# Seven block products for eight in a pooled-attention and feed-forward kernel, with the second weight matrix read from DRAM at every step

## The chip, the cores and the metric

The kernel runs on one core of a Trainium2 chip. The metric is the device time of one execution in microseconds (us); the time of a kernel is the median of several executions. Engines are named as the profile names them: PE is TensorE's matrix array, PEld its weight loads, DVE VectorE, ACT ScalarE, POOL GpSimd, SP SyncE, which issues all DMAs here.

## What is computed

Attention over keys and values that are averaged in groups of eight, then a feed-forward layer with a squared ReLU:

```python
k_p = k.reshape(B, H, Sp, pool, D).mean(axis=3)      # B, H, S, D = 8, 8, 576, 64; pool = 8
v_p = v.reshape(B, H, Sp, pool, D).mean(axis=3)
scores = scale * np.matmul(q, k_p.transpose(0, 1, 3, 2))
...
x = np.ascontiguousarray(attn_out.transpose(0, 2, 1, 3)).reshape(B * S, H * D)   # 4608 x 512
h = np.maximum(x @ w_in, 0.0)                        # w_in 512 x 2048
return (h * h @ w_out)                               # w_out 2048 x 512
```

All tensors are float32. The weights arrive as 64-bit numbers, which the kernel converts itself.

## The kernel before

The 4608 tokens are cut into 12 chunks of 384 (`CH`). A chunk has 16 steps (`NFC`), one for each block of 128 hidden units. One step multiplies the chunk's x by one block of w_in (`hidden`: 12 matmuls of 128x128 weights with 384 columns, tiles h), takes ReLU and square into r (`activate`), splits r into a high and a low float32r part (`split_hidden`: gh by a cast on ACT, gl by a subtraction on DVE), and multiplies the parts of two steps ago (`LAG`) by a block of w_out into three banks o that collect a whole chunk (`project`: 9 matmuls of 512 columns, three for each bank). Every float32 product of chunks 1 to 11 is made of three float32r products: high x high, high x low, low x high. That is why h reads xh and xl, and both halves of a weight tile w_i. Both weight matrices stay in SBUF, in 33 tiles of the tag "w".

After the last step of a chunk `store` copies the three banks through tiles ob (`OB`, 3 buffers) and sends them out.

The attention of the next chunk runs beside that, in four pairs of heads, p = 0 to 3, each a sequence of stages: `turn_q`, `split_q` (tiles st: two casts on ACT, two subtractions on DVE), `scores` (tiles sps on PE, copied to sc by ACT, the column maximum mx by POOL), `exponents` (subtraction, Exp on ACT, the sums tot by POOL), four small DMAs that turn the sums into reciprocals rb (rs, rc, rr, rd), and `weigh_values` (av on PE, scaled by rb on DVE, split into xh and xl). A table gives the step of each stage: `STEADY` holds the first step of each pair of heads, counted from the chunk's own first step, and the distances of the nine stages.

Engines run in the order in which the loop at the end of the program records instructions: for a step first `hidden`, then the attention's matmuls, `project`, `split_hidden`, the remaining stages of the table, the loads, and last `activate` and `store`. Nothing is reordered afterwards. An instruction that waits therefore holds up everything behind it on its engine. SP is such a queue too. The lines to find are `split_q` (L375), `scores` (L384), `exponents` (L409), `hidden` (L552), `split_hidden` (L579), `project` with `store` (L589) and the loop (L740).

Of the kernel before, what the change touches and what calls it, by code (L numbers as in the profile page):

```python
# [37 lines left out]
def pooled_attn_relu2_ffn(  # L38
# [45 lines left out]
    SPLIT = 6  # L84


    STEADY = ((-22, -18, -14, -10), (-1, 0, 1, 3, 4, 5, 6, 7, 8))
    KV0 = -39
    EARLY = ((-16, -13, -10, -7), (0, 1, 2, 3, 5))

    NKT = H * SP_ // QT
# [422 lines left out]

    x0 = []

    def split_x0():
        xts[0] = [sb.tile([P, NPAIR, CH], F32R, name=f"{x}_0", tag=x, bufs=2) for x in ("xh", "xl")]
        for i, x in enumerate(x0):
            split(*(t[:, 2 * i:2 * i + 2] for t in xts[0]), x)  # L520

    def weigh_values(c, p):

        if p == 0 and c == 0:
            x0.extend(w_tile(F32, f"x_{c}_{i}")[:, :, :CH] for i in range(2))
# [26 lines left out]
    def hidden(c, fc):  # L552
        hp = ps_h.tile([P, 512], F32, name=f"h_{c}_{fc}", tag="h")
        cb, o = fc * P // WC, fc * P % WC
        prods = []
        for cc in range(NCC):
            key, cols = ("i", cb, cc // 2 * 2), slice(cc % 2 * WC + o, cc % 2 * WC + o + P)
            if c == 0 and fc < SPLIT:
                prods += [(wf[key][:, cols], x0[cc // 2][:, cc % 2, :])]
            else:  # L560
                prods += [(wt[key][:, w, cols], xts[c][x][:, cc, :]) for w, x in ((0, 0), (0, 1), (1, 0))]
        for i, (w, x) in enumerate(prods):
            PE.matmul(hp[:, :CH], lhsT=w, rhs=x, start=i == 0, stop=i == len(prods) - 1)
# [23 lines left out]
    accs = {}  # L587

    def project(c, fc):  # L589
        if fc == 0:  # L590
            accs[c] = [ps_o.tile([P, 512], F32, name=f"o_{c}_{t}", tag=f"o{t}") for t in range(NTT)]
        g, key = gts.pop((c, fc)), ("o", fc)
        for t in range(NTT):
            tt = slice(t * P, (t + 1) * P)
            if c == 0:
                prods = [(g[:, tt], wf[key])]
            else:
                prods = [(g[x][:, tt], wt[key][:, w, :]) for x, w in ((0, 0), (0, 1), (1, 0))]
            for i, (a, w) in enumerate(prods):
                PE.matmul(accs[c][t], lhsT=a, rhs=w, start=fc == 0 and i == 0, stop=fc == NFC - 1 and i == len(prods) - 1)  # L600

        def store():
# [5 lines left out]
        return store if fc == NFC - 1 else None  # L608


    steps = [(c, fc) for c in range(NCH) for fc in range(NFC)]
# [99 lines left out]
    def kv_steps(b, s):
# [9 lines left out]
    ready = {0, 1}  # L721
    stages = (turn_q, split_q, scores, exponents, send_sums, fetch_sums, reciprocals, fetch_reciprocals, weigh_values)
    for c in range(1, NCH):
        first, offsets = EARLY if c == 1 else STEADY
        names = (transpose_q, token_scores, token_normalise, token_turn, weigh_values) if c == 1 else stages
        for b, _, _ in segments(c):
            if b not in ready:
# [7 lines left out]
                at(s + d, f, c, p)  # L735


    last = (to_float32, split_weights)
    on_pe = (transpose_k, transpose_q, scores, token_scores, token_turn, weigh_values)
    for s in range(-PRO, len(steps) + LAG):  # L740
        todo = work.get(s, [])
        activate = hidden(*steps[s]) if 0 <= s < len(steps) else None
        later = [f(*a) for f, a in sorted(((f, a) for f, a in todo if f in on_pe), key=lambda x: x[0] is weigh_values)]
        store = project(*steps[s - LAG]) if s >= LAG else None
        if 0 <= s - 1 < len(steps):
            split_hidden(*steps[s - 1])
# [12 lines left out]
        for f in (activate, store):  # L759
            if f:  # L760
                f()

# [29 lines left out]
```

## Time and profile before

| | |
|---|---|
| median of 3 executions | 944.36 us (944.16 to 945.4) |
| the profiled execution | 946.16 us |
| its span, first to last instruction | 944.4 us |
| mean granted clock of TensorE | 0.997 |
| matmuls, weight loads | 4776, 4776 |
| DMA | 68.06 MB, 72 GB/s on average |

The page gives busy time by engine, then groups of instructions: operation, output<-inputs, shape, count | busy us, mean ns of one | idle time of the engine ahead of them and what ended it. The chain lists what ended last, in order of time. In a table of windows each row is a stretch of time with the busy us of PE, PEld, DVE, ACT and POOL, the granted clock, the DMA engines' share and GB/s. All work is recorded through one helper, L34, so groups are told apart by their tiles.

### The profile page before, as it was taken

To read this page: it belongs to the slowest core of one execution; us is meant where nothing else is said; L and a number is where in the kernel's file an instruction comes from. 1 tells how busy PE (TensorE), PEld (TensorE's weight loads), DVE (VectorE), ACT (ScalarE), POOL (GpSimd) and SP (SyncE) were. 2 spreads that over 40 slices of the span, in tenths; PEclk is the share of its full clock that TensorE was granted. 3 is DMA by queue.
4 is the path that set the end of the run, shared out by engine and by line. 5 is a ranking of instruction groups with operands and counts; after the bars stand their busy time and mean duration, and the time that the engine had idled before them with its cause. 6 is when DMAs were issued, how large, how long until landed. Compare 5 with 4: busy or idle time off the path is not lost.

```text
span 944.4 us, 13423 instructions
## 1 busy us (share of the span) xinstructions
PE 929.4 (98%) x4776; PEld 785.4 (83%) x4776; DVE 598.3 (63%) x1020; ACT 434.4 (46%) x903; POOL 352.9 (37%) x215
## 2 busy tenths in 40 slices
PE   7899999999999999999999999999999999999998
PEld 6556668888888888888888888888888888888997
DVE  7988896766655576776765576676765555553221
ACT  3888766654434344344435334434434443432222
POOL 3820144435344443534443443435344443530000
PEclk9999999999999999999999999999999999999999
DMA  9975213223112113223211023223311101100000
GB/s 258 319 241 144 73 40 104 60 69 99 43 30 68 36 50 95 68 73 87 63 36 52 19 68 87 51 75 91 70 41 40 53 18 28 50 10 10 34 1 33
DMA packets 124682, 68.06 MB, mean 72 GB/s; under 512 B 95800, under 2 KB 105224, under 8 KB 124616
## 3 DMA queue, kind: packets, MB, share of 16 engines
q1 hardware_dynamic: 124616, 67.22, 26.3%
q8 instruction: 37, 0.61, 0.3%
q14 instruction: 29, 0.24, 0.1%
HBM read 55.73 MB, written 11.45 MB: 71 GB/s over the span
## 4 chain that ended last, share of the span: by engine, by line
PE 88%; DMA 4%; DVE 3%; POOL 2%; ACT 2%; issue 1%; SPq 0%; DVEq 0%; ACTq 0%
PE o L34 41%; PE h L34 40%; PE av L34 3%; PE sps L34 3%; POOL v L34 2%; DMA k<-in_k_dram 1%; DMA v<-in_v_dram 1%; DVE wf_o L34 1%; DVE wf_i L34 1%; POOL vp L34 1%; DMA raw_i<-in_moe_w_in_dram 1%; DMA vv<-in_v_dram 1%; DVE tm L34 1%; ACT te L34 1%; DVE w_i L34 0%
## 5 line engine op out<-in xcount | busy, mean ns | idle before, releaser
L34 PE MATMUL h<-xh,w_i 128*128 128x384 f32 x1488 | 417.1, 341 | 0.0
L34 PE MATMUL o<-w_o,gh 128*128 128x512 f32 x1056 | 333.9, 397 | 0.0
L34 PEld LDWEIGHTS h<-xh,w_i 128*128 128x128 f32 x1488 | 272.6, 188 | 10.7 <-issue 2.2
L34 POOL PARTITION_ALL_REDUCE tot<-sc x80 | 202.2, 2574 | 188.6 <-issue 178.4
L34 PE MATMUL h<-xl,w_i 128*128 128x384 f32 x744 | 249.8, 336 | 0.0
L34 PEld LDWEIGHTS o<-w_o,gh 128*128 128x128 f32 x1056 | 193.1, 188 | 51.6 <-issue 16.5
L34 POOL PARTITION_ALL_REDUCE mx<-sc x80 | 114.8, 1483 | 285.3 <-ACT sc L34 279.3
L34 DVE TENSOR_TENSOR gl<-r,gh 128x384 fp32r<-128x384 f32 x176 | 137.0, 779 | 114.4 <-ACT gh L34 114.4
L34 PE MATMUL o<-w_o,gl 128*128 128x512 f32 x528 | 208.8, 395 | 0.0
L34 DVE TENSOR_TENSOR r<-r 128x384 f32<-128x384 f32 x160 | 100.8, 630 | 132.8 <-ACT r L34 131.0
L34 ACT ACTIVATE r<-h 128x384 f32<-128x384 f32 x192 | 94.4, 492 | 136.0 <-PE h L34 135.0
L34 ACT CAST gh<-r 128x384 fp32r<-128x384 f32 x176 | 90.4, 514 | 130.3 <-DVE r L34 129.8
L34 PEld LDWEIGHTS h<-xl,w_i 128*128 128x128 f32 x744 | 139.7, 188 | 10.6 <-issue 3.1
L34 PEld LDWEIGHTS o<-w_o,gl 128*128 128x128 f32 x528 | 99.1, 188 | 22.2
L34 ACT CAST xh<-rb 128x384 fp32r<-128x384 f32 x40 | 20.5, 513 | 120.2 <-DVE rb L34 120.2
L34 ACT ACTIVATE sc<-sc 72x384 f32<-72x384 f32 x80 | 39.7, 525 | 47.0 <-DVE sc L34 47.0
L34 DVE TENSOR_TENSOR rb<-av,rb 128x384 f32<-128x384 f32 x40 | 22.3, 557 | 40.5 <-PE av L34 40.5
L34 DVE TENSOR_TENSOR st<-qt,st 64x384 fp32r<-64x384 f32 x80 | 44.2, 553 | 3.5 <-ACT st L34 1.0
L34 ACT COPY sc<-sps 72x384 f32<-72x384 f32 x80 | 34.1, 477 | 26.6 <-PE sps L34 26.6
L34 PE MATMUL av<-sc,vp 72*64 72x384 f32 (+1 forms) x256 | 43.8, 426 | 2.3 <-ACT sc L34 2.3
L34 PE MATMUL o<-wf_o,r 128*128 128x512 f32 x96 | 44.6, 601 | 0.0
L34 DVE TENSOR_REDUCE kp<-k 96x64 f32<-96x512 f32 x42 | 43.6, 1038 | 0.1
(82 smaller groups left out, 709.6 us busy)
## 6 DMA issues: line engine op xcount, KB each, us to landing
k<-in_k_dram SPq DMA_DIRECT2D x48, 192.0 KB
out_dram<-ob SPq DMA_DIRECT2D x36, 256.0 KB
raw_i<-in_moe_w_in_dram SPq DMA_DIRECT2D x16, 512.0 KB
raw_o<-in_moe_w_out_dram SPq DMA_DIRECT2D x16, 512.0 KB
rb<-rd SPq DMA_DIRECT2D x80, 96.0 KB
v<-in_v_dram SPq DMA_DIRECT2D x36, 192.0 KB
q<-in_q_dram SPq DMA_DIRECT2D x112, 48.0 KB
q<-in_q_dram SPq DMA_DIRECT2D x96, 24.0 KB
```

Source lines behind the costliest of these rows:

```text
L34: return lambda *a, **k: self.tc.keep_in_program_order(f(*a, **k))
```

## The change

From chunk 3 (`SC`) on the product of w_in and x is made by Strassen's scheme in Winograd's form. The weights are four blocks A11, A12, A21, A22 (halves of the hidden units by halves of the model dimension), x four blocks B11 to B22 (halves of the model dimension by halves of the chunk's tokens, 192 columns each). Seven block products take the place of eight: A11·B11, A12·B21, S2·T2, S1·T1, S3·T3, S4·B22, A22·T4, where S1 to S4 are sums of weight blocks and T1 to T4 differences of x blocks. A block product is six matmuls of 192 columns (`product`). Two steps together make one pair q: 128 hidden units of the first half and 128 of the second. `first_half` has four products, `second_half` three. Results are gathered in r1 and r2: partial sums stay in the PSUM banks pc (chain), pd and pe, and ACT and DVE copy and add between products.

The sums S are built once, in steps 30 to 57, and stay in SBUF (16 tiles). For them the parts of w_out move out: `evict` writes each of the 16 tiles to DRAM, and from chunk 2 (`MC`) on `stream` reads the one that a step needs, two steps ahead, 512 KB each. `project` runs three steps behind from chunk 2 on, and its three thirds, one for each bank, are put between the products. The differences T and the splits of the seven operands stand in the last three steps ahead of a chunk and in its first. In `exponents` the subtraction moves from DVE to POOL for chunks from 3 on. The stages of the attention move two steps earlier, ob has two buffers for three, and the tag "w" 32 for 33.

```diff
-    LAG, QL = 2, 5
+    HB = CH // 2
+    NQD = NFC // 2
+    SC, MC = 3, 2
+    LAG, FLAG, QL = 2, 3, 5
...
-    STB, SCB, LD, OB = 1, 2, 4, 3
+    STB, SCB, LD, OB, XB, KPB = 1, 2, 4, 2, 8, 2
+    BUILD, RING = (30, 37, 44, 51), 2
...
-    STEADY = ((-22, -18, -14, -10), (-1, 0, 1, 3, 4, 5, 6, 7, 8))
+    STEADY = ((-24, -20, -16, -12), (-1, 0, 1, 3, 4, 5, 6, 7, 8))
...
-        return wts.tile([P, 2, 512], dt, name=name, tag="w", bufs=2 * NFC + 1)
+        return wts.tile([P, 2, 512], dt, name=name, tag="w", bufs=2 * NFC)
...
-            DVE.tensor_tensor(sc[:, i], sc[:, i], mx[i], op=ALU.subtract)
+            (GP if c >= SC else DVE).tensor_tensor(sc[:, i], sc[:, i], mx[i], op=ALU.subtract)
...
+            if c >= SC:
+                DVE.tensor_tensor(xf[c][p // 2][:, p % 2, :], av[:, :CH], rb, op=ALU.mult)
+                return
...
+        elif name == "T2":
+            GP.tensor_tensor(tmp[c], block(c, "B22"), tmp[c], op=ALU.subtract)
...
+    def operand(c, name):
+        src = {"T1": tmp.get(c), "T2": tmp.get(c), "T3": block(c, "B12"), "T4": block(c, "B21")}.get(name)
+        t = ops[c, name] = x_tile(f"{name}_{c}").rearrange("p x (a n) -> p x a n", a=2)
+        split(t[:, 0], t[:, 1], block(c, name) if src is None else src)
...
+    def product(c, q, w, x, bank, start):
+        g, o = q // 2, q % 2 * P
+        t = wt[("s", int(w[1]), g) if w[0] == "S" else ("i", g + 4 * (w[1] == "2"), 2 * (w[2] == "2"))]
+        prods = [(t[:, i, k * WC + o:k * WC + o + P], ops[c, x][:, j, k, :])
+                 for k in range(2) for i, j in ((0, 0), (0, 1), (1, 0))]
+        for i, (a, b) in enumerate(prods):
+            PE.matmul(bank[:, :HB], lhsT=a, rhs=b, start=start and i == 0, stop=i == len(prods) - 1,
+                      skip_group_check=not start)
...
+    def parts(c, f):
...
+        split(gh, gl, gts[c, f])
...
+    def rest(c, q):
+        r2 = gts[c, q + NQD]
+        ACT.activation(r2[:, HB:], r2[:, HB:], AF.Relu)
+        ACT.activation(r2, r2, AF.Square)
+        parts(c, q + NQD)
+
+    def first_half(c, q, before, out_groups, on_array):
+        chain = ps_h.tile([P, 512], F32, name=f"pc_{c}_{q}", tag="h")
+        product(c, q, "A11", "B11", chain, True)
+        r1 = result_tile(c, q)
+        ACT.copy(r1[:, :HB], chain[:, :HB])
+        if before:
+            parts(*before)
+        next(out_groups, None)
+        other = ps_h.tile([P, 512], F32, name=f"pd_{c}_{q}", tag="h")
+        product(c, q, "A12", "B21", other, True)
+        DVE.tensor_tensor(r1[:, :HB], other[:, :HB], r1[:, :HB], op=ALU.add)
+        product(c, q, "S2", "T2", chain, False)
+        ACT.copy(r1[:, HB:], chain[:, :HB])
+        last = ps_a.tile([P, 512], F32, name=f"pe_{c}_{q}", tag="a")
+        product(c, q, "S1", "T1", last, True)
+        r2 = result_tile(c, q + NQD)
+        ACT.copy(r2[:, HB:], last[:, :HB])
+        next(out_groups, None)
+        later = on_array()
+        next(out_groups, None)
+        if before:
+            rest(*before)
...
+    def second_half(c, q, out_groups, on_array):
+        chain, last, r1, r2 = quads.pop((c, q))
+        product(c, q, "S3", "T3", chain, False)
+        DVE.tensor_tensor(r2[:, HB:], chain[:, :HB], r2[:, HB:], op=ALU.add)
+        later = on_array()
+        next(out_groups, None)
+        next(out_groups, None)
+        product(c, q, "S4", "B22", last, False)
+        next(out_groups, None)
+        product(c, q, "A22", "T4", chain, False)
+
+        def finish():
+            DVE.tensor_tensor(r1[:, HB:], last[:, :HB], r1[:, HB:], op=ALU.add)
+            DVE.scalar_tensor_tensor(r1, r1, 0.0, r1, op0=ALU.max, op1=ALU.mult)
+            ACT.activation(r2[:, :HB], chain[:, :HB], AF.Relu)
...
+    def evict(f):
+        d = scratch[f] = dram.tile([P, 2, 512], F32, name=f"wd_{f}", tag=f"wd_{f}", bufs=1)
+        load(d, wt["o", f].bitcast(F32))
+
+    def stream(c, f):
+        t = streamed[c, f] = w_tile(F32R, f"ws_{c}_{f}")
+        load(t.bitcast(F32), scratch[f])
...
+        w_o = wf[key] if c == 0 else wt[key] if c < MC else streamed.pop((c, fc))
...
+    for s, (c, f) in projects.items():
+        if c >= MC:
+            at(s - RING, stream, c, f)
+    for g, s in enumerate(BUILD):
+        for stage in range(7):
+            at(s + stage, build, g, stage)
+    for c in range(SC, NCH):
+        s = c * NFC
+        for d, f, name in ((-9, difference, "T1"), (-3, operand, "B11"), (-3, difference, "T3"), (-2, operand, "B21"),
+                           (-2, operand, "T1"), (-2, difference, "T2"), (-1, operand, "T2"), (-1, operand, "T3"),
+                           (-1, operand, "B22"), (-1, difference, "T4"), (0, operand, "T4")):
+            at(s + d, f, c, name)
```

On PE a step of before, here the second of chunk 6, starts with the 12 matmuls of h; w_i are tiles of w_in, xh and xl the parts of x:

```order
L34 MATMUL h_6_1_5130<-xh_6_4457,w_i_0_0_1309 128x384 [waits Activation_49]
L34 MATMUL h_6_1_5130<-xl_6_4458,w_i_0_0_1309 128x384
L34 MATMUL h_6_1_5130<-xh_6_4457,w_i_0_0_1309 128x384 x2
L34 MATMUL h_6_1_5130<-xl_6_4458,w_i_0_0_1309 128x384
L34 MATMUL h_6_1_5130<-xh_6_4457,w_i_0_0_1309 128x384
L34 MATMUL h_6_1_5130<-xh_6_4457,w_i_0_2_1312 128x384
L34 MATMUL h_6_1_5130<-xl_6_4458,w_i_0_2_1312 128x384
L34 MATMUL h_6_1_5130<-xh_6_4457,w_i_0_2_1312 128x384 x2
L34 MATMUL h_6_1_5130<-xl_6_4458,w_i_0_2_1312 128x384
L34 MATMUL h_6_1_5130<-xh_6_4457,w_i_0_2_1312 128x384
```

Now the first step of a pair (the last of chunk 5) starts so; ws are the streamed tiles of w_out, w_s2 and w_s1 the sums S2 and S1, and the wait named is for another engine's semaphore:

```order
L34 MATMUL pc_5_7_5902<-B11_5_4899,w_i_3_0_727 128x192 x6
L34 MATMUL o_5_0_5246<-ws_5_13_5844,gh_5_13_5831 128x512 [waits DMAHW4_49]
L34 MATMUL o_5_0_5246<-ws_5_13_5844,gh_5_13_5831 128x512
L34 MATMUL o_5_0_5246<-ws_5_13_5844,gl_5_13_5832 128x512
L34 MATMUL pd_5_7_5918<-B21_5_4967,w_i_3_2_781 128x192 [waits Activation_49]
L34 MATMUL pd_5_7_5918<-B21_5_4967,w_i_3_2_781 128x192 x5
L34 MATMUL pc_5_7_5902<-T2_5_5019,w_s2_3_3533 128x192 [waits Activation_49]
L34 MATMUL pc_5_7_5902<-T2_5_5019,w_s2_3_3533 128x192 x5
L34 MATMUL pe_5_7_5933<-T1_5_4970,w_s1_3_3419 128x192 [waits PE_49]
L34 MATMUL pe_5_7_5933<-T1_5_4970,w_s1_3_3419 128x192 x5
L34 MATMUL o_5_1_5247<-ws_5_13_5844,gh_5_13_5831 128x512 x2
L34 MATMUL o_5_1_5247<-ws_5_13_5844,gl_5_13_5832 128x512
```

Twelve matmuls of 384 columns have become groups of six with 192, o's thirds stand between them, and three of the groups wait for ACT or for PE's own earlier work.

On ACT, around the change from chunk 5 to chunk 6, before: r and gh of two steps, then the attention's Exp (sc) for chunk 7:

```order
L34 ACTIVATE r_5_15_5093<-h_5_15_5048 128x384 [waits Activation_49]
L34 CAST gh_5_15_5118<-r_5_15_5093 128x384 [waits DVE_49]
L34 ACTIVATE r_6_0_5127<-h_6_0_5096 128x384 [waits PE_49,Activation_49]
L34 CAST gh_6_0_5152<-r_6_0_5127 128x384 [waits DVE_49]
L34 ACTIVATE sc_7_1_5084<-sc_7_1_5084 72x384 [waits DVE_49] x2
L34 ACTIVATE r_6_1_5178<-h_6_1_5130 128x384 [waits PE_49,Activation_49]
```

Now, around the same place, from the gh of a second result on:

```order
L34 CAST gh_5_14_5950<-r_5_14_5818 128x384 [waits Activation_49]
L34 CAST B21_6_5960<-xf_6_2_5585 128x384
L34 CAST T1_6_5963<-t_6_5527 128x384
L34 ACTIVATE sc_7_1_5884<-sc_7_1_5884 72x384 [waits Pool_49] x2
L34 CAST T2_6_6011<-t_6_5527 128x384
L34 CAST T3_6_6014<-xf_6_0_5080 128x384
L34 CAST B22_6_6017<-xf_6_2_5585 128x384 [waits PE_49]
L34 ACTIVATE r_5_15_5940<-pc_5_7_5902 128x192 [waits PE_49]
```

Five casts of operands and the Exp of chunk 7, which now waits for POOL, stand ahead of the r of pc_5_7, which the bank's next product waits for.

On ACT at the stores of chunk 5, before:

```order
L34 COPY ob_5_0_5181<-o_5_0_4462 128x512 [waits PE_49]
L34 COPY ob_5_1_5184<-o_5_1_4463 128x512 [waits DMAHW6_49,PE_49]
L34 COPY ob_5_2_5187<-o_5_2_4464 128x512 [waits DMAHW7_49,PE_49]
L34 CAST gh_6_1_5222<-r_6_1_5178 128x384 [waits DVE_49]
L34 CAST xh_7_5203<-rb_7_0_5156 128x384 [waits DMAHW4_49,DMAHW3_49,DVE_49]
L34 CAST st_7_2_5232<-qt_7_2_5167 64x384 x2
L34 ACTIVATE r_6_2_5237<-h_6_2_5190 128x384 [waits PE_49,Activation_49]
```

and now, from the second copy on:

```order
L34 COPY ob_5_1_6219<-o_5_1_5247 128x512 [waits DMAHW4_49,PE_49]
L34 COPY ob_5_2_6222<-o_5_2_5248 128x512 [waits DMAHW3_49,PE_49,Activation_49]
L34 ACTIVATE sc_7_2_6143<-sc_7_2_6143 72x384 [waits Pool_49] x2
L34 ACTIVATE r_6_9_6195<-pc_6_1_6157 128x192 [waits PE_49]
L34 COPY r_6_2_6286<-pc_6_2_6279 128x192 [waits DVE_49,PE_49]
L34 CAST gh_6_1_6288<-r_6_1_6164 128x384 [waits DVE_49]
L34 COPY r_6_2_6286<-pc_6_2_6279 128x192 [waits PE_49]
L34 COPY r_6_10_6317<-pe_6_2_6310 128x192 [waits DVE_49,PE_49]
L34 ACTIVATE r_6_9_6195<-r_6_9_6195 128x192
L34 ACTIVATE r_6_9_6195<-r_6_9_6195 128x384 [waits Activation_49]
L34 CAST gh_6_9_6332<-r_6_9_6195 128x384 [waits Activation_49]
L34 CAST st_7_3_6340<-qt_7_3_6267 64x384 x2
```

The third copy (ob_5_2) now waits for DMAHW3 (the store of ob_5_0), where it waited for a store of the chunk before. The last rows show the st casts, which stood alone behind xh, behind two copies, r twice and gh.

More of the change, by code (lines that the diff above doesn't have):

```diff
@@ L515, in pooled_attn_relu2_ffn, with x_tile @@
     x0 = []
+    def x_tile(name):
+        return sb.tile([P, 2, CH], F32R, name=name, tag="x", bufs=XB)
     def split_x0():
-        xts[0] = [sb.tile([P, NPAIR, CH], F32R, name=f"{x}_0", tag=x, bufs=2) for x in ("xh", "xl")]
-        for i, x in enumerate(x0):
-            split(*(t[:, 2 * i:2 * i + 2] for t in xts[0]), x)
+        xts[0] = [x_tile(f"x_0_{p}") for p in range(NPAIR)]
+        for p, t in enumerate(xts[0]):
+            split(t[:, 0, :], t[:, 1, :], x0[p // 2][:, p % 2, :])
     def weigh_values(c, p):
@@ L577, in hidden, with block, difference @@
         return activate
+    xf, ops, tmp = {}, {}, {}
+    def block(c, name):
+        x = xf[c][name[1] == "2"]
+        return x[:, :, HB:] if name[2] == "2" else x[:, :, :HB]
+    def difference(c, name):
+        if name == "T1":
+            t = tmp[c] = sb.tile([P, 2, HB], F32, name=f"t_{c}", tag="t", bufs=1)
+            GP.tensor_tensor(t, block(c, "B12"), block(c, "B11"), op=ALU.subtract)
+        elif name == "T2":
+            GP.tensor_tensor(tmp[c], block(c, "B22"), tmp[c], op=ALU.subtract)
+        elif name == "T3":
+            GP.tensor_tensor(block(c, "B12"), block(c, "B22"), block(c, "B12"), op=ALU.subtract)
+        else:
+            GP.tensor_tensor(block(c, "B21"), block(c, "B21"), tmp[c], op=ALU.subtract)
@@ new lines, in operand, with build, keep @@
+    def operand(c, name):
+        src = {"T1": tmp.get(c), "T2": tmp.get(c), "T3": block(c, "B12"), "T4": block(c, "B21")}.get(name)
+        t = ops[c, name] = x_tile(f"{name}_{c}").rearrange("p x (a n) -> p x a n", a=2)
+        split(t[:, 0], t[:, 1], block(c, name) if src is None else src)
+    def build(g, stage):
+        a11, a12, a21, a22 = (wt["i", g + 4 * r, 2 * k] for r in range(2) for k in range(2))
+        hi, lo = (lambda t: t[:, 0, :].bitcast(F32)), (lambda t: t[:, 1, :].bitcast(F32))
+        def keep(n, src):
+            t = wt["s", n, g] = w_tile(F32R, f"w_s{n}_{g}")
+            split(t[:, 0, :], t[:, 1, :], src)
+        if stage == 0:
+            us[g] = [half_tile("u", f"u{i}_{g}") for i in range(2)]
+        u1, u2 = us[g]
+        if stage == 0:
+            DVE.tensor_tensor(u1, hi(a21), lo(a21), op=ALU.add)
+        elif stage == 1:
+            DVE.tensor_tensor(u2, hi(a22), lo(a22), op=ALU.add)
+            GP.tensor_tensor(u2, u1, u2, op=ALU.add)
+        elif stage == 2:
+            keep(1, u2)
+            DVE.tensor_tensor(u1, hi(a11), u1, op=ALU.subtract)
+        elif stage == 3:
+            GP.tensor_tensor(u2, u2, hi(a11), op=ALU.subtract)
+            GP.tensor_tensor(u2, u2, lo(a11), op=ALU.subtract)
+            DVE.tensor_tensor(u1, u1, lo(a11), op=ALU.add)
+        elif stage == 4:
+            keep(2, u2)
+            keep(3, u1)
+        elif stage == 5:
+            GP.tensor_tensor(u2, hi(a12), u2, op=ALU.subtract)
+            DVE.tensor_tensor(u2, u2, lo(a12), op=ALU.add)
+        else:
+            keep(4, u2)
@@ new lines, in first_half @@
+    def first_half(c, q, before, out_groups, on_array):
[20 more added lines that the diff above has]
+            rest(*before)
+        quads[c, q] = (chain, last, r1, r2)
+        return later
@@ L595, in project @@
             if c == 0:
[L596 removed]
+                prods = [(g[:, tt], w_o)]
             else:
[L598 removed]
+                prods = [(g[x][:, tt], w_o[:, w, :]) for x, w in ((0, 0), (0, 1), (1, 0))]
             for i, (a, w) in enumerate(prods):
                 PE.matmul(accs[c][t], lhsT=a, rhs=w, start=fc == 0 and i == 0, stop=fc == NFC - 1 and i == len(prods) - 1)
+            yield
         def store():
@@ L606, in store @@
                 dma(out[c * CH + t * P:c * CH + (t + 1) * P, :], ob)
-        return store if fc == NFC - 1 else None
+        if fc == NFC - 1:
+            store()
     steps = [(c, fc) for c in range(NCH) for fc in range(NFC)]
@@ L723, in pooled_attn_relu2_ffn @@
     for c in range(1, NCH):
-        first, offsets = EARLY if c == 1 else STEADY
+        first, offsets = EARLY if c == 1 else THIRD if c < SC else STEADY
         names = (transpose_q, token_scores, token_normalise, token_turn, weigh_values) if c == 1 else stages
@@ L735, in pooled_attn_relu2_ffn @@
                 at(s + d, f, c, p)
+    order = {c: list(range(NFC)) if c < SC else [q + NQD * r for q in range(NQD) for r in range(2)] for c in range(NCH)}
+    projects = {c * NFC + i + (LAG if c < MC else FLAG): (c, f) for c in range(NCH) for i, f in enumerate(order[c])}
+    for s, (c, f) in projects.items():
[10 more added lines that the diff above has]
+            at(s + d, f, c, name)
@@ L738, in pooled_attn_relu2_ffn, with on_array @@
     last = (to_float32, split_weights)
     on_pe = (transpose_k, transpose_q, scores, token_scores, token_turn, weigh_values)
-    for s in range(-PRO, len(steps) + LAG):
+    for s in range(-PRO, max(projects) + 1):
         todo = work.get(s, [])
[L742 to L746, printed above, removed]
+        def on_array():
+            return [f(*a) for f, a in sorted(((f, a) for f, a in todo if f in on_pe), key=lambda x: x[0] is weigh_values)]
+        groups = project(*projects[s]) if s in projects else iter(())
+        activate = finish = None
+        c, fc = steps[s] if 0 <= s < len(steps) else (0, 0)
+        if c < SC:
+            activate = hidden(c, fc) if 0 <= s < len(steps) else None
+            later = on_array()
+            for _ in groups:
+                pass
+            if 0 <= s - 1 < len(steps) and steps[s - 1][0] < SC:
+                split_hidden(*steps[s - 1])
+            if s == len(steps):
+                parts(NCH - 1, NQD - 1)
+                rest(NCH - 1, NQD - 1)
+        elif fc % 2 == 0:
+            qd = fc // 2
+            pc, pq = (c, qd - 1) if qd else (c - 1, NQD - 1)
+            if pc < SC:
+                split_hidden(pc, NFC - 1)
+            later = first_half(c, qd, (pc, pq) if pc >= SC else None, groups, on_array)
+        else:
+            later, finish = second_half(c, fc // 2, groups, on_array)
@@ L758, in pooled_attn_relu2_ffn @@
         issue_loads()
-        for f in (activate, store):
+        for _ in groups:
+            pass
+        for f in (activate, finish):
             if f:
```

39 lines of the change are left out of this document (26 added, 13 removed).

## The prediction

> **What bounds the kernel now.** I read the page's busy line first, then the chain that ended last, then the stages.
>
> ```profile
> PE 929.4 (98%) x4776; PEld 785.4 (83%) x4776; DVE 598.3 (63%) x1020; ACT 434.4 (46%) x903; POOL 352.9 (37%) x215
> PE 88%; DMA 4%; DVE 3%; POOL 2%; ACT 2%; issue 1%; SPq 0%; DVEq 0%; ACTq 0%
> ```
> ```profile
> 200.00:260.00 60.00, 60.00 (x305) 52.06 (x304) 39.70 (x65) 27.53 (x58) 23.78 (x13) 1.00 0.27 68
> 500.00:560.00 60.00, 60.00 (x321) 53.02 (x320) 33.67 (x58) 25.01 (x52) 26.34 (x14) 1.00 0.17 44
> ```
>
> TensorE is busy for the whole of a steady stage at granted clock 1.00, while VectorE has a third to a half of its time free, and ScalarE and GpSimd over half. There is a matmul for every weight load. The chain in order of time gives one period:
>
> ```profile
> 512.15 0.80 PE av L34 x8
> 512.95 2.28 PE o L34 x9
> 515.23 2.11 PE h L34 x12
> 517.33 0.71 PE sps L34 x8
> 518.04 2.12 PE o L34 x9
> 520.16 2.10 PE h L34 x12
> 522.26 2.08 PE o L34 x9
> ...
> 530.64 0.80 PE av L34 x8
> ```
>
> Four steps take 530.64 − 512.15 = 18.49 us: four h groups of 2.10, four o groups of 2.08, one attention pair (0.80 + 0.71, and 0.20 more in the o group behind av). Nothing else stands in it. So two things can change the time: what a group costs on TensorE, and gaps that the change opens.
>
> **Term 1, the products.** Two steps have 24 h matmuls of 384 columns, 2 × 2.10 = 4.20 us. Now they have 7 products of 6 matmuls, 42 of 192 columns. By columns that is 8064 for 9216, one eighth less. But each matmul still loads 128 columns of weights. The trace has one place where a 192-column matmul is followed by such a load: the end of a scores group.
>
> ```profile
> 277.63 0.25 PE L34 MATMUL sps<-st,kl 128*72 128x192 f32 x1
> 277.72 0.25 PE L34 MATMUL sps<-st,kh 128*72 128x192 f32 x1
> 277.81 0.65 PE L34 MATMUL o<-w_o,gh 128*128 128x512 f32 x2
> 278.29 0.39 PE L34 MATMUL o<-w_o,gl 128*128 128x512 f32 x1
> ```
> ```profile
> 277.72 0.30 PEld L34 LDWEIGHTS o<-w_o,gh 128*128 128x128 f32 x2
> ```
>
> With 72-column weights behind it a 192-column matmul takes 277.72 − 277.63 = 0.09 us. The last one starts at 277.72 and the third o matmul at 278.29; two o matmuls take 2 × 2.08 / 9 = 0.46, so the last scores matmul held the array for 0.57 − 0.46 = 0.11 us. The loads say the same: two loads last 0.30 us together and one alone 0.19, so the second began 0.11 after the first. [...] I take 0.11 for each of the 42: 4.62 us, **+0.42 us** per two steps. Eight such pairs in each of chunks 3 to 11 are 72 pairs: **+30 us**. If the load were hidden, 42 × 0.09 = 3.78, −0.42 per pair: −30 us. Those are the ends; the row at 277.72 has the new shape exactly, so I take its value.
>
> [...]
>
> **Terms 2 to 4, the waits.** The new order has TensorE wait for ScalarE and VectorE inside a step. These rows price what is queued there:
>
> ```profile
> L34 ACT CAST gh<-r 128x384 fp32r<-128x384 f32 x176 | 90.4, 514 | 130.3 <-DVE r L34 129.8
> L34 ACT CAST st<-qt 64x384 fp32r<-64x384 f32 x80 | 40.7, 509 | 1.0
> L34 ACT ACTIVATE sc<-sc 72x384 f32<-72x384 f32 x80 | 39.7, 525 | 47.0 <-DVE sc L34 47.0
> L34 ACT COPY x<-av 128x384 f32<-128x384 f32 x4 | 1.9, 479 | 2.9 <-PE av L34 2.9
> L34 ACT COPY kf<-kps 128x288 f32<-128x288 f32 x4 | 1.4, 383 | 6.1 <-PE kps L34 6.1
> L34 ACT COPY ob<-o 128x512 f32<-128x512 f32 x36 | 20.9, 587 | 6.9 <-PE o L34 3.2
> L34 DVE TENSOR_TENSOR gl<-r,gh 128x384 fp32r<-128x384 f32 x176 | 137.0, 779 | 114.4 <-ACT gh L34 114.4
> L34 DVE TENSOR_TENSOR st<-qt,st 64x384 fp32r<-64x384 f32 x80 | 44.2, 553 | 3.5 <-ACT st L34 1.0
> L34 DVE TENSOR_TENSOR rb<-av,rb 128x384 f32<-128x384 f32 x40 | 22.3, 557 | 40.5 <-PE av L34 40.5
> L34 DVE TENSOR_SCALAR rr<-rc 96x8 f32<-96x8 f32 x40 | 10.5, 263 | 0.0
> L34 DVE RECIPROCAL rr<-rr 96x8 f32<-96x8 f32 x40 | 8.0, 199 | 1.4
> L34 DVE TENSOR_TENSOR w_o<-wf_o,w_o 128x512 fp32r<-128x512 f32 x16 | 13.6, 863 | 2.5 <-ACT w_o L34 2.5
> L34 POOL TENSOR_TENSOR v<-v 72x256 f32<-72x256 f32 x8 | 12.1, 1506 | 1.1 <-DMA v<-in_v_dram 1.1
> L34 POOL TENSOR_TENSOR k<-k 96x256 f32<-96x256 f32 x6 | 4.3, 724 | 6.5 <-DMA k<-in_k_dram 6.5
> ```
> ```profile
> 522.10 0.62 PE L34 MATMUL o<-w_o,gh 128*128 128x512 f32 x2
> ...
> 522.36 0.49 ACT L34 ACTIVATE r<-h 128x384 f32<-128x384 f32 x1 [2.02 <-PE h L34]
> ```
>
> Estimates from them: 192 columns on ScalarE 0.29 us (479 and 383 ns are 1 ns a column apart); ScalarE starts 0.26 after the array has gone on (522.36 − 522.10). gl I take at 0.56, as the like subtraction rb (0.779 has waits behind GpSimd in it); a GpSimd subtraction of 384 columns at 1.0 (724 ns for 256, scaled), with 2.2 from the v row as its upper end.
>
> Clock of a first step, from its first product: A11·B11 ends at 0.66, an o third (0.69) at 1.35, A12·B21 at 2.01, S2·T2 at 2.67, S1·T1 at 3.33, o at 4.02, av (1.00, in every second pair) and o at 4.72 or 5.72. The second step is 4.06 without scores.
>
> *Term 2, scores.* ScalarE's copy of S1·T1 starts at 3.59; behind it stand copy, relu, square and gh (0.29 + 0.29 + 0.53 + 0.51), done 5.21, then two st casts, 5.72 and 6.23. VectorE does gl until 5.77, xf until 6.33, the two st subtractions until 6.88 and 7.43. TensorE, in order, is through S3·T3 at 5.72 + 0.66 = 6.38 and reaches the scores: it waits 0.50 for the first head, and after it 0.2 to 0.4 for the second. I take 0.8 us. Four times for each of chunks 5 to 11 and twice for chunk 4: 30 × 0.8 = **24 us** (0 to 36, with gl at 0.779). Before, this wait hardly existed:
>
> ```profile
> PE sps L34 <- DVE st L34: 0.6, 1, 0.6
> ```
>
> *Term 3, chunk change.* Two steps ahead of a new chunk, gh ends at 5.21, gl at 5.77, rr at 6.23, then VectorE's B21 and T1 at 6.79 and 7.35. GpSimd's T2 waits for that T1 (8.35) and holds up the two exponent subtractions (10.35), for which ScalarE's Exp waits (10.88). Behind Exp stand the casts of T2, T3 and B22 (12.42) and the relu that frees the bank for A12·B21 (12.71). TensorE wants it at 4.72 + 4.06 + 0.66 + 0.69 = 10.13: 2.6 us. Chunks 4 to 10 have it, for chunk 11 has no next attention: **18 us** (0, if ScalarE gets there earlier, to 43 with three GpSimd operations at 2.2).
>
> *Term 4, stores.* With two ob buffers for three, the third copy of a chunk waits until the first store has landed.
>
> ```profile
> 939.99 1.72 SPq L34 DMA_DIRECT2D out_dram<-ob  x3
> ```
> ```profile
> SPq L787 <- DMA out_dram<-ob: 1.6, 1, 1.6
> ```
>
> A landing comes 1.6 us after the last issue, an issue takes about 0.4. In step 2 of a chunk gh ends at 5.21, the copies at 5.80 and 6.38. SP issues rd (after rr, 6.23), ws, then the store: 7.43, landed 9.03, third copy done 9.62. TensorE wants the first o bank at 5.38 (waits 0.42) and, after two o thirds and S4·B22, the third at 7.84 (waits 1.78): 2.2 us, nine times: **20 us** (0 to 34, if the 512 KB read ahead of it delays the store by its own 1.3). At the very end it adds 1.6 + 0.4 = **2 us**.
>
> **What costs nothing.** The four builds are 36 VectorE operations of about 0.86 (31 us) over some 130 us of chunks 2 and 3, where VectorE has 20 of 60 us free; uncovered, up to 8 us. The weights now read in every step are 512 KB; at the 392 GB/s of the rows below that is 1.3 us of a 4.7 us step, with DMA shares of 0.17 to 0.27 beside it, issued two steps early. Chunks 0 to 2 keep their TensorE work.
>
> **Sum.** The profiled span is 944.4 us in an execution of 946.16; the median of the runs is 944.36, so I add to 944.4: 30 + 24 + 18 + 20 + 2 = 94, **1038 us**.
>
> **Rivals.** *The waits are hidden* (other work of ScalarE and VectorE runs earlier than my clock has it): terms 1 and the end alone, 976. For it: both engines have slack; against: the order fixes what stands ahead.
>
> *The loads hide*, the side of faster: −30, with no waits 914. It decides below 4.20 / 42 = 0.100 us per product matmul; with the 62 us of waits it still gives about 976, so faster needs both, hidden loads and waits under 30 us. Against it stands the row at 277.72.
>
> *The clock drops.* TensorE has no gaps now. Early in the trace it has one:
>
> ```profile
> 32.00:34.00 2.00, 0.58 (x4) 0.29 (x3) 2.00 (x4) 2.00 (x4) 2.00 (x1) 1.00 1.07 370
> 34.00:36.00 2.00, 2.00 (x7) 0.79 (x6) 1.90 (x7) 0.80 (x2) 1.84 (x4) 0.74 0.98 376
> 36.00:38.00 2.00, 2.00 (x13) 1.97 (x13) 2.00 (x5) 0.26 (x2) 1.84 (x4) 0.50 1.05 392
> ```
>
> After a wait of 1.4 us the clock is 0.74 and 0.50 for two slices: 0.52 + 1.00 = 1.5 us lost. At 16 waits of 2 us and more that is +24: 1062, or 1085 with longer GpSimd times. [...]
>
> **Chances.** Forecast 0.57, waits hidden 0.18, loads hidden 0.13 (half of it faster), clock 0.12. The range 976 to 1085 leaves out the loads' faster half and some of each end. Faster 0.06, within 0.2% (all that a measurement of this kernel can tell from no change) 0.01, slower 0.93.
>
> **What would show it.** Right: product matmuls 0.11 us apart, with a load each; TensorE idle before sps (VectorE st), before the A12·B21 of a chunk's first pair (ScalarE r) and before o (ScalarE ob). Wrong: intervals of 0.09, or a TensorE without idle time in a chunk.

## The result, and the profile after

The changed kernel takes **1513.59 us** (median of 4 executions, 1505.97 to 1515.06) against 944.88 for the kernel before on the same chip: a ratio of 1.5996, 95% interval 1.5936 to 1.6056. That is 569 us more, where 94 were forecast; it lies far above the range.

The page of the changed kernel, busy time and the chain that ended last, then two windows of it (columns as before: PE, PEld, DVE, ACT, POOL, granted clock, DMA share, GB/s):

```profile
PE 1126.0 (74%) x6072; PEld 927.2 (61%) x6072; DVE 642.5 (42%) x1157; ACT 523.7 (35%) x1236; POOL 487.1 (32%) x339
PE 40%; issue 18%; DMA 11%; POOL 10%; DVE 10%; ACT 9%; SPq 2%; POOLq 0%; DVEq 0%; ACTq 0%
```
```profile
200.00:260.00 60.00, 35.83 (x142) 30.29 (x143) 20.90 (x36) 19.20 (x40) 21.24 (x13) 0.76 0.36 106
600.00:700.00 100.00, 73.32 (x399) 60.56 (x397) 40.19 (x71) 29.87 (x76) 33.99 (x22) 0.83 0.39 103
```

Every engine is now idle for a good part of the time, TensorE too, and no engine has become the bound. Compared with before, TensorE is busy for 197 us more (1126.0 for 929.4) and idle for 372 us more. Of the 197, term 1 forecast 30; most of the rest I put down to the granted clock, 0.861 in this execution for 0.997, an estimate by subtraction. 18% of the chain is "issue": an engine stands still and nothing that the profile records ends its wait. The waits of the changed kernel say on which engine (us in total, times, longest):

```profile
ACT sc L34 <- POOL sc L34: 192.7, 56, 17.0
POOL tot L34 <- ACT r L34: 156.6, 25, 6.9
POOL sc L34 <- issue: 154.1, 21, 8.0
...
PE pd L34 <- ACT r L34: 81.7, 14, 11.7
...
PE sps L34 <- DVE st L34: 77.9, 42, 13.3
...
POOL u L34 <- issue: 68.6, 9, 8.4
...
POOL xf L34 <- issue: 66.7, 9, 8.5
PE pc L34 <- DVE r L34: 64.4, 13, 8.9
```

GpSimd waits about 7 us each time, ahead of sc, xf and u alike: the operations that the change moved there. GpSimd's timeline in the kernel before and in the changed one shows the pattern (start, us, operation, count, idle time before it):

```profile
518.53 2.83 POOL L34 PARTITION_ALL_REDUCE mx<-sc  x2 [6.26 <-ACT sc L34]
525.76 5.01 POOL L34 PARTITION_ALL_REDUCE tot<-sc  x2 [4.40 <-issue]
```
```profile
578.51 1.95 POOL L34 TENSOR_TENSOR sc<-sc,mx 72x384 f32<-72x384 f32 x2 [7.08 <-issue]
587.31 5.05 POOL L34 PARTITION_ALL_REDUCE tot<-sc  x2 [6.86 <-ACT r L34]
593.23 2.84 POOL L34 PARTITION_ALL_REDUCE mx<-sc  x2 [0.87 <-ACT sc L34]
603.06 2.30 POOL L34 TENSOR_TENSOR sc<-sc,mx 72x384 f32<-72x384 f32 x2 [7.00 <-issue]
611.65 5.05 POOL L34 PARTITION_ALL_REDUCE tot<-sc  x2 [6.29 <-issue]
```

Before, reductions follow reductions, and the gaps between them are waits for input. That holds for tot too, although its 4.40 us are labelled "issue": it starts at 525.76, just behind the first of ScalarE's two Exp, which take 0.5 us each:

```profile
525.08 1.00 ACT L34 ACTIVATE sc<-sc 72x384 f32<-72x384 f32 x2 [1.09 <-DVE sc L34]
```

Now a TENSOR_TENSOR stands between mx and tot, with 7 us of nothing ahead of it and over 6 behind. The second gap is labelled "ACT r" in one row and "issue" in another: the label does not name the cause. ScalarE's rows show that this time tot's input was long there:

```profile
579.53 0.53 ACT L34 ACTIVATE sc<-sc 72x384 f32<-72x384 f32 x1
580.49 0.52 ACT L34 ACTIVATE sc<-sc 72x384 f32<-72x384 f32 x1 [0.44 <-POOL sc L34]
```

The two Exp are done at 580.1 and 581.0; tot starts at 587.3. Over the whole trace I count 112 changes of kind: 56 from a reduction to an elementwise operation, never under 6.83 us apart (median 7.39), and 56 back, never under 5.78 (median 6.18). Operations of one kind can follow each other without a gap: 186 of 219 such pairs are under 0.2 us apart. The trace also has 226 MODIFY_POOL_CONFIG instructions on GpSimd's sequencer for 4 before: two at each of the 112 changes, none between operations of one kind, two at the start. So the gaps stand at each change and in both directions. What GpSimd does in them no run here shows; "reload" in the expectations below is my name for such a gap.

How TensorE comes to stand still for it shows at a change of chunk, all engines in order of time:

```profile
558.02 0.40 PE L34 MATMUL o<-ws,gl 128*128 128x512 f32 x1
...
561.74 0.98 POOL L34 TENSOR_TENSOR xf<-xf,t 128x384 f32<-128x384 f32 x1 [6.96 <-issue]
562.76 0.51 ACT L34 CAST T<-xf 128x384 fp32r<-128x384 f32 x1 [11.00 <-POOL xf L34]
...
563.30 0.56 DVE L34 TENSOR_TENSOR T<-xf,T 128x384 fp32r<-128x384 f32 x1 [8.38 <-ACT T L34]
563.78 0.35 DVE L34 TENSOR_TENSOR r<-pc,r 128x192 f32<-128x192 f32 x1
...
564.28 1.57 PE L34 MATMUL pc<-T,w_i 128*128 128x192 f32 x6 [5.86 <-DVE r L34]
```

GpSimd's gap holds ScalarE's cast, that holds VectorE's queue, in which the sum r stands that frees TensorE's bank. TensorE loses 5.86 us, and its label names only the last link, VectorE.

By the starts of the output copies a steady chunk takes 129.6 us where it took 73.9; chunk 1, in which the attention of chunk 3 begins, 113.4 for 72.0; chunk 2, with the builds, 182.5 for 73.9; the last one, without attention of a next chunk, 63.2 for 62.8.

### The profile page after: what moved, and what is told of

The parts are those of the page before. It is cut to its first block, busy times and chain, and to the rows that moved or that the text cites. A ratio compares the mean times of both kernels' runs of the same rounds, so it can differ in the third digit from the quotient of the medians.

```text
span 1513.0 us, 17157 instructions
## 1 busy us (share of the span) xinstructions
PE 1126.0 (74%) x6072; PEld 927.2 (61%) x6072; DVE 642.5 (42%) x1157; ACT 523.7 (35%) x1236; POOL 487.1 (32%) x339
## 4 chain that ended last, share of the span: by engine, by line
PE 40%; issue 18%; DMA 11%; POOL 10%; DVE 10%; ACT 9%; SPq 2%; POOLq 0%; DVEq 0%; ACTq 0%
PE o L34 14%; PE pc L34 10%; DMA ws<-wd 5%; PE pe L34 5%; POOL tot L34 4%; ACT r L34 4%; PE pd L34 4%; PE h L34 3%; DMA out_dram<-ob 3%; DVE st L34 3%; POOL sc L34 2%; PE sps L34 2%; ACT gh L34 2%; SPq L34 2%; DVE gl L34 1%
## 5 line engine op out<-in xcount | busy, mean ns | idle before, releaser
L34 PE MATMUL o<-ws,gh 128*128 128x512 f32 x960 | 345.1, 443 | 82.3 <-DMA ws<-wd 44.1
L34 PEld LDWEIGHTS o<-ws,gh 128*128 128x128 f32 x960 | 175.2, 210 | 125.5 <-issue 44.8
L34 PE MATMUL o<-ws,gl 128*128 128x512 f32 x480 | 204.7, 426 | 0.0
L34 PE MATMUL h<-x,w_i 128*128 128x384 f32 x504 | 113.8, 380 | 50.7 <-ACT r L34 50.7
L34 PE MATMUL pc<-T,w_s 128*128 128x192 f32 x864 | 133.2, 295 | 10.9 <-ACT r L34 10.8
L34 PEld LDWEIGHTS pc<-T,w_s 128*128 128x128 f32 x864 | 128.8, 215 | 18.1 <-ACT r L34 11.5
L34 PEld LDWEIGHTS h<-x,w_i 128*128 128x128 f32 x504 | 100.4, 212 | 63.2 <-ACT r L34 55.4
L34 PE MATMUL pd<-B,w_i 128*128 128x192 f32 x432 | 76.6, 325 | 81.7 <-ACT r L34 81.7
L34 PE MATMUL pc<-T,w_i 128*128 128x192 f32 x432 | 70.7, 307 | 64.5 <-DVE r L34 64.4
L34 PEld LDWEIGHTS o<-ws,gl 128*128 128x128 f32 x480 | 100.3, 209 | 24.7
L34 ACT ACTIVATE r<-r 128x384 f32<-128x384 f32 (+1 forms) x176 | 81.0, 460 | 3.3
```

Of the source, the lines that this page charges most:

```text
L34: return lambda *a, **k: self.tc.keep_in_program_order(f(*a, **k))
```

## The experiments

**One part of the change at a time, on the kernel before.**

*Only the exponents' subtraction on GpSimd:*

```diff
-            DVE.tensor_tensor(sc[:, i], sc[:, i], mx[i], op=ALU.subtract)
+            (GP if c >= 3 else DVE).tensor_tensor(sc[:, i], sc[:, i], mx[i], op=ALU.subtract)
```

> The kernel before with one thing of the change: the exponent subtraction on GpSimd for chunks from 3 on, 72 changes of kind. Reload theory: one pair of heads takes GpSimd 2.9 + 7 + 2 + 7 + 5 = 24 us where four steps of TensorE take 18.5, 36 pairs, so about 5.5 us each: 944 + 200 = 1140 us. Rival theory (the operation costs its own 1 us): within 10 us of 944.

Measured: 1105.19 us, ratio 1.1697 (1.1674 to 1.1721). That is somewhat less than the 1140 of the first theory and far outside the second. One engine name in one line costs 160 us, without products and without streamed reads. Its timeline of GpSimd has the same two gaps, here labelled with a load that has nothing to do with it:

```profile
587.13 1.94 POOL L34 TENSOR_TENSOR sc<-sc,mx 72x384 f32<-72x384 f32 x2 [6.99 <-DMA q<-in_q_dram]
594.95 5.19 POOL L34 PARTITION_ALL_REDUCE tot<-sc  x2 [5.87 <-ACT r L34]
```

*Only the 192-column matmuls* (each h group as two halves, with the same weights loaded for each):

```diff
+        for n in range(0, CH, CH // 2 if c >= 3 else CH):
+            cols = slice(n, n + CH // 2 if c >= 3 else CH)
...
+                PE.matmul(hp[:, cols], lhsT=w, rhs=x[:, cols], start=i == 0, stop=i == len(prods) - 1)
```

> The kernel before, with each h matmul of 384 columns from chunk 3 on made as two of 192, each with its own 128-column weight load; nothing else. If a load takes the array's 0.11 us: 48 x 0.11 = 5.28 us for two steps in place of 4.20, 72 times +1.08: 944 + 78 = 1022 us. If loads hide behind 0.09 us: 48 x 0.09 = 4.32, 944 + 9 = 953 us.

Measured: 1025.57 us, ratio 1.0854 (1.0833 to 1.0876). Over 144 steps that is 0.56 us each, so 24 matmuls take 2.10 + 0.56 = 2.66 us, 0.111 each: the price of term 1.

*Only two output buffers* (`OB = 2`), and *only the streamed w_out* (`evict`, `stream` and the reads from chunk 2 on):

> The kernel before with two buffers for the output copies instead of three, nothing else. If a chunk's third copy waits for the first store and PE waits behind it, as term 4 of the prediction has it (2.2 us a chunk): 944 + 11 x 2.2, 964 to 970 us. If the wait is hidden by the products: 944 to 947 us. In the changed kernel this wait was 4.5 us, so 990 us and more would say that two buffers alone cost that much, without the streamed reads beside the stores.

> The kernel before with w_out's parts written to DRAM in chunk 1 and read back for each step from chunk 2 on (two steps ahead, into the 16 slots that they leave), nothing else. If the streamed reads cost nothing by themselves: 944 to 948 us, with the stores' landing longer than before's 2.04 us. If the reads are late for their matmuls or hold the queue by themselves: 2 to 4 us a chunk, 965 to 985 us.

Measured: 948.35 us (1.0038, 1.0025 to 1.0051) and 945.47 us (1.0007, 0.9996 to 1.0018). With two buffers the third copies wait 21.4 us on ScalarE in the whole run, but TensorE waits 1.2 for them. The streamed reads alone cost nothing that can be measured. Both together:

> The kernel before with two output buffers and w_out's parts read back from DRAM together, which alone cost 3.5 and 0.6 us. In the kernel with all arithmetic on VectorE the third copy's wait cost PE 4.5 us a chunk, with a step's read issued just ahead of the store. If it is the read beside the store that makes the wait long: PE waits for the third copy in chunks 3 to 11, 2 to 4.5 us each and half the clock behind it, 965 to 1000 us. If it is the place of the last output products in the changed order: no more than the two alone, 948 to 953 us.

Measured: 953.38 us (1.0078, 1.0058 to 1.0098), 0.4 us above the second theory and well below the first. It is 8.1 us more than before, twice the sum of the two alone. Its waits:

```profile
ACT ob L34 <- DMA out_dram<-ob: 28.3, 10, 4.7
...
PE o L34 <- ACT ob L34: 2.6, 2, 1.8
```

ScalarE waits up to 4.7 us for the store, TensorE 2.6 us in the whole run: in the old order other matmuls stand ahead of the one that needs the third bank. So neither the buffers nor the reads make term 4 dear in the old order. What does so in the new one is not settled. The matmul that needs the third bank comes sooner there; and in chunks 2 to 9 a read of w_out is issued half a microsecond ahead of the first store, which here happens in no chunk. The first stores land 4.6 us after their issue there and 2.8 here (medians). No run changes one of the two alone.

**Taking the elementwise work off GpSimd in the changed kernel.** All the operations (`GP.tensor_tensor` to `DVE.tensor_tensor` in `exponents`, `difference` and `build`), and the exponents' alone:

> The changed kernel with every elementwise operation that it gave to GpSimd (exponent subtractions, differences, builds) back on VectorE, in the same places. Reload theory (each change of GpSimd between TENSOR_TENSOR and PARTITION_ALL_REDUCE costs it 6 to 8 us, 112 changes in the run, and TensorE waits for what is behind): GpSimd keeps one change, the time falls from 1513 to about 1040, where the other terms of the prediction put it, clock above 0.97. Rival theory (products, ScalarE and VectorE waits, the streamed reads and the slower clock make the 570 us): it stays above 1350.

> The changed kernel with the exponent subtractions alone back on VectorE; differences and builds stay on GpSimd, and 65 of 111 added reload rows stay. Reload theory: GpSimd needs per chunk 4 x 8 us of reductions, 4 us of differences and 6 reloads of 7 us, 78 us, about what TensorE needs, so the steady chunks come near 85 us for 130, in all 1100 to 1250 us, with waits bunched at the chunk changes. Rival theory: above 1400.

Measured: 1192.43 us (ratio to before 1.2618, 1.2597 to 1.2639) and 1343.94 us (1.4224, 1.4196 to 1.4253). VectorE gets more work and the kernel is 321 us faster: over half of the 569. Of the changes of kind only the one at the kernel's start is left. The exponents alone give 170 of it; the differences and builds, moved back on top of that, the other 151. Neither expectation was met in full: 1343.94 lies between the two theories, and 1192 at a clock of 0.948 is well above the 1040 at over 0.97 of the first. So GpSimd is not all of it. TensorE's three longest waits in the kernel with all arithmetic on VectorE, in 460 us of steady chunks (540 to 1000):

```profile
PE sps L34 <- DVE st L34: 21.0, 25, 2.9
PE o L34 <- ACT ob L34: 18.6, 8, 4.8
PE o L34 <- DMA ws<-wd: 18.0, 10, 3.2
```

**One of these waits taken away at a time,** from the kernel with all arithmetic on VectorE. The third copy in a slot of the loads' ring:

```diff
-                ob = sb.tile([P, DM], F32, name=f"ob_{c}_{t}", tag="ob", bufs=OB)
+                ob = sb.tile([P, DM], F32, name=f"ob_{c}_{t}", **(dict(tag="ob", bufs=OB) if t < 2 else dict(tag="ld", bufs=LD)))
```

> The kernel with all arithmetic back on VectorE (1192 us), and the third output copy of a chunk in a slot of the loads' ring, so that it no longer waits for the first store. It lost some 15 us a steady chunk in waits of PE (4.7 of it for this copy) and some 10 to the granted clock. If the lowered clock follows the waits: the wait and its share of the clock go, 9 x (4.7 + 3.0) = 69 us, about 1123 us at a clock above 0.96. If the clock has another cause (more matmuls in a given time): only the wait goes, about 1150 us at 0.95. If another wait takes its place: over 1175 us.

Measured: 1144.04 us (1.2116, 1.2065 to 1.2166), 48 us less, at a clock of 0.966 for 0.948. The clock is that of the first theory, the time nearer to that of the second (1150).

The wait for ws is a question of SyncE's queue. Its rows in the kernel with all arithmetic on VectorE, and the matmul that needed the last of these reads:

```profile
854.83 0.30 SPq L34 DMA_DIRECT2D rc<-rs  x1
855.23 0.38 SPq L34 DMA_DIRECT2D ws<-wd  x1
864.69 0.30 SPq L34 DMA_DIRECT2D rd<-rr  x1
865.04 0.42 SPq L34 DMA_DIRECT2D v<-in_v_dram  x1
865.51 0.42 SPq L34 DMA_DIRECT2D ws<-wd  x1
```
```profile
870.10 0.70 PE L34 MATMUL o<-ws,gh 128*128 128x512 f32 x2 [1.88 <-DMA ws<-wd]
```

For 9 us the queue stands at rd, which waits for VectorE's rr; the read behind it leaves 4.6 us before its use, about a landing (4.2 us median in that trace). So the third copy freed, and the read recorded at the head of its step:

```diff
+        for f, a in todo:
+            if f is stream:
+                stream(*a)
+        issue_loads()
         groups = project(*projects[s]) if s in projects else iter(())
```

> As the kernel with the third copy freed (1144 us), and each step's read of w_out is put ahead of the step's other transfers in SyncE's queue, where it stood behind the reciprocals' transfer, which waits there for VectorE's rr. PE's waits for ws were 20 us in 460 us, 4.1 us a chunk. If the read is late because of its place in the queue: the waits go with a share of the clock, 9 x (4 to 6.6) = 37 to 60 us, 1085 to 1107 us. If the read is late because the transfer itself takes too long (4.4 us landing): no change, 1135 to 1150 us.

Measured: 1125.33 us (1.1922, 1.1885 to 1.1959): 19 us less, where 37 to 60 were expected. The wait for ws is gone from TensorE's list, but sps now waits longer (it was 23.5 us):

```profile
PE sps L34 <- DVE st L34: 31.9, 26, 2.9
PE pd L34 <- ACT r L34: 2.7, 5, 0.6
```

A part of the time won was given back to the next wait. Casting q one step earlier (offsets -2, -1 for `turn_q` and `split_q`, from -1, 0), alone and on top of the two others:

> The kernel with all arithmetic back on VectorE (1192 us), and the turning and the casting of q one step earlier from chunk 3 on, so that the scores' matmuls no longer wait for VectorE's st (4.8 us a steady chunk over four waits). If the wait goes with its share of the clock: 9 x (4.8 + 3.0) = 70 us, about 1122 us. If the wait only moves (VectorE has the same work in the same chunk, and the products' operands or sums come later instead): over 1175 us.

> Third copy freed, reads of w_out ahead, and the casting of q one step earlier. Alone on the kernel with three fixed waits of PE left, the earlier casts moved the wait to other tiles. If the remaining time is the waits (23.5 us for st in 460 us, 4.8 a chunk, and their clock): 9 x (4.8 to 7.5) = 43 to 68 us less than without the earlier casts, 1020 to 1060 us, which is the sum of the matmuls (975) and a chunk change. If VectorE's own work sets the time: within 10 us of the kernel without the earlier casts. In no case below 976, the matmuls alone.

Measured: 1187.18 us (1.2556, 1.2533 to 1.2578) and 1139.66 us (1.2069, 1.2040 to 1.2098): nearly nothing alone, as the second theory has it, and 14 us worse than without it on top of the others, which neither theory had. The wait for st is gone, and others have come, in the second kernel:

```profile
PE sps L34 <- DVE xf L34: 17.2, 12, 2.1
PE pd L34 <- ACT r L34: 15.0, 12, 2.7
```

TensorE's gaps add up to 39 us in 460 with the earlier casts and without them; the in-order queues of ScalarE and VectorE hold the same work in another order. What is worse is the clock, 0.943 for 0.957 (last section).

Last, the waiting time filled: 16 matmuls on the identity ahead of the matmul that waits for the third copy.

> The kernel with all arithmetic back on VectorE (1192 us), and 16 matmuls on the identity whose result nobody reads, put ahead of the matmul that waits 4.5 us for the third copy in each chunk from 4 on. If the lowered clock follows PE's idle stretches (half the clock in the 3 to 4 us behind such a gap in the trace): work added makes it faster, 8 x 1.6 to 2.0 us, 1176 to 1180 us. If the clock falls with the work done: slower, 1192 to 1230 us.

Measured: 1191.94 us (1.2617, 1.2583 to 1.2651), the same as without them. That is the lower end of the second theory, but the clock did not fall with the work: it was 0.958 for 0.948. In the chunk that begins at 837 us in both traces the gap of 4.51 us shrank to 0.89 and the clock stayed full behind it, but the scores that follow, which had waited 0.36 us for st, now wait for 1.66 (TensorE's timeline of the filled kernel):

```profile
854.71 0.40 PE L34 MATMUL sps<-st,kl 128*72 128x384 f32 x1 [1.66 <-DVE st L34]
```

Here a full clock bought nothing, for VectorE's st was the next thing late.

## Why the prediction was wrong

**The step that failed is the price of GpSimd's operations**, in the estimates ahead of the terms ("a GpSimd subtraction of 384 columns at 1.0 [...], with 2.2 from the v row as its upper end") and so in the sum, where the exponents' move to GpSimd cost something only at the chunk change (term 3). The duration was right, as the costliest groups of the changed kernel have it:

```profile
L34 POOL TENSOR_TENSOR sc<-sc,mx 72x384 f32<-72x384 f32 x72 | 73.1, 1030 | 168.3 <-issue 154.1
```

It lasts 1.03 us (724 ns for 256 columns scale to 1.09, not 1.0); but with it come the gaps, 7.4 us ahead and 6.2 behind. The k and v rows that bounded it stand at the kernel's start, where GpSimd does nothing but elementwise work. The place to look was the order of operations on GpSimd: 48 elementwise ones, then reductions only. No rival had this mechanism. Undoing all the moves to GpSimd gave back 321 us, and making the exponents' move alone cost 160.

**Term 1** was right: the six matmuls of a product take 0.67 us at full clock in the changed kernel, 0.112 each (586.00 to 586.67 to 587.34, its timeline of TensorE):

```profile
586.00 0.83 PE L34 MATMUL pc<-T,w_s 128*128 128x192 f32 x6
586.67 0.84 PE L34 MATMUL pe<-T,w_s 128*128 128x192 f32 x6
587.34 0.64 PE L34 MATMUL o<-ws,gh 128*128 128x512 f32 x2
```

The kernel that does only this cost the 0.11 us per matmul that was forecast. That the loads hide, at 0.09 each, is refuted, and with it the way to a faster kernel that the prediction saw.

**Term 2** had the right mechanism and about half the size: with GpSimd cleared of the elementwise work TensorE waits 45.3 us for st in the whole run (43 waits), where 24 were forecast and 36 at the upper end. An earlier cast removed the wait but not the time.

**Term 3** was right at its own place and missed the places that cost. At the A12·B21 of a chunk's first pair TensorE waits 1.3 to 1.7 us for ScalarE's r in chunks 4 to 8 of the changed kernel, for 2.6 forecast. But of the 81.7 us of pd 59 stand before the A12·B21 of the seventh pair of chunks 3 to 9, where ScalarE's Exp waits for GpSimd's subtraction, and 56 of the 64.4 of pc before the A22·T4 of the first pair of chunks 3 to 10, as in the rows above. Both come from the gaps of GpSimd: with all arithmetic on VectorE the waits of pd and pc nearly vanish (under 2 us in those 460).

**Term 4** forecast 2.2 us a chunk; the changed kernel shows 4.5 before the third bank alone,

```profile
579.65 1.22 PE L34 MATMUL o<-ws,gh 128*128 128x512 f32 x2 [4.46 <-ACT ob L34]
```

and the freed copy gave 48 us back, not 20. A chunk's first store lands later than the prediction took it from the kernel's quiet end: 4.6 us after its issue (median), for 2.0 before, which are the prediction's 1.6 and 0.4. It takes 4.4 to 4.8 us in chunks 2 to 9, with a read of w_out issued just ahead, and 2.0 to 2.7 in the other four. The prediction named this delay for the upper end of the term, as 1.3 us (nine times that on top of 20 is 32, not 34). The clock falls behind the gap as well.

**"What costs nothing"** failed at two places. The builds' 36 operations on VectorE take 28 us in the changed kernel, so they were sized right (31 forecast). That they would be covered was wrong at least where GpSimd's part of the builds is on VectorE too, 52 operations in 47 us, 31 us of them in chunk 2. That chunk before, and with the third copy freed and reads ahead as well:

```profile
213.20:287.10 73.90, 73.90 (x377) 63.94 (x376) 46.15 (x77) 31.01 (x65) 31.55 (x17) 1.00 0.23 58
```
```profile
223.90:325.10 101.20, 87.53 (x438) 74.18 (x436) 76.53 (x123) 40.63 (x90) 36.96 (x18) 0.90 0.47 133
```

VectorE has 30.4 us more in it, and the chunk is 27 us longer, not "up to 8": half of that in gaps of TensorE, half in its matmuls at a clock of 0.90. No run has the builds as the prediction has them, without GpSimd's gaps. And the reads of w_out are late, not by their size but by their place in SyncE's queue, behind a transfer that waits for VectorE: 19 us.

**The clock** was a rival at 0.12, for 24 us, and it is part of every wait above. It is not small: 1 minus the granted clock comes to 210 us in the changed kernel (0.861 over 1513 us), some of them while TensorE stood still, and to 62 with all arithmetic on VectorE (0.948 over 1191). Most of it went with the gaps of GpSimd; what a full clock alone would give back was not measured.

What the 569 us are, then, taken away in this order: 321 the elementwise work on GpSimd, 48 the third copy, 19 the reads' place in the queue, each with the clock that it cost. 180 are left in the fastest of these versions: 13 us in chunk 1 (why, no run shows), 27 in chunk 2, 15 to 22 in each of chunks 3 to 8 (95.2 us for 73.9 in chunk 8), 13 and 4 in the two behind. Of that chunk's 21 us TensorE's gaps are 8 and the lowered clock 4 (39.1 and 20.4 us in 460; the latter by adding up 1 minus the clock over 4-us windows); term 1 forecast 8 x 0.42 = 3.4. Some 6 us a chunk I could not assign.

## What to carry to other kernels

Before an operation is moved to another engine, ask what stands next to it there: its own duration is no price where the engine stops at each change between two kinds of work. Here two subtractions of 1 us each between cross-partition reductions cost over 13 us of GpSimd's time besides their own. Leaving them on VectorE was tried; grouping them by kind was not.

A wait with "issue" as its releaser can be a cost of the engine itself, but neither the label nor a constant length shows it: in the kernel before tot waits for "issue" 39 times past 100 us, mostly 4.4 to 4.6 us, and every time tot starts 0.15 us behind the end of an Exp, which is what it waits for. What shows it is an input that has long been ready, and a gap that stays while its label changes. And freeing one wait in a chain of in-order queues can only move it, as when the wait for ws went and that of sps grew from 23.5 to 31.9 us: take waits away one at a time and read the next list.

## What the runs showed of the hardware

GpSimd's change between PARTITION_ALL_REDUCE and TENSOR_TENSOR in the changed kernel: at least 6.83 us towards TENSOR_TENSOR (median 7.39) and 5.78 back (median 6.18), on every one of 112 occasions. The kernel before has a like gap once, at its start, 7.3 us for "issue" ahead of `ones`; the changed kernel has 0.3 us there, so what that gap is stays open.

A longer gap of TensorE is here mostly followed by half the clock, for 3.4 us or more, so it costs some 1.7 us or more besides its length. In the kernel with the third copy freed, from 700 to 1000 us, all five gaps of 2.3 us or more have it, one of two at 1.7 us, and none of thirteen from 0.6 to 1.3 us. It is no fixed rule: in the nine traces with such gaps, past 150 us, 87 of 97 gaps of 2.3 to 3.4 us have it, and all of 90 longer ones; one of 3.0 us passes at full clock in the kernel with the exponents alone back on VectorE. And the slow stretch can be much longer: in the changed kernel 25 of its 57 slow stretches last 3.4 us, the others 4.5 to 23.9; in the kernel with the earlier casts on top, behind a gap of 2.65 us,

```profile
816.00:818.00 2.00, 2.00 (x11) 2.00 (x11) 1.39 (x4) 0.67 (x2) 0.00 (x0) 0.50 0.18 29
818.00:820.00 2.00, 2.00 (x9) 1.60 (x7) 0.64 (x2) 1.01 (x4) 0.00 (x0) 0.50 0.30 48
820.00:822.00 2.00, 2.00 (x6) 0.47 (x6) 0.61 (x2) 0.77 (x2) 0.00 (x0) 0.50 0.82 233
822.00:824.00 2.00, 2.00 (x7) 1.72 (x8) 0.50 (x1) 0.00 (x0) 0.00 (x0) 0.50 0.87 237
```

TensorE is busy without a break and still at half the clock for some 10 us. What keeps it there was not tried.
